# Casts of token weights handed out at other places, a second PSUM bank for outputs, and four tiles given over to float32 values

## The chip, the cores and the metric

The program runs on one core of one Trainium2 chip. The metric is the device time of one execution in microseconds (us). An execution is summed up below by its median over several runs; a profiled execution has a span (first to last instruction) and, a little longer, a time of its own.

A core has a matmul engine (PE) with its weight loads (PEld), the vector engine (DVE), the scalar engine (ACT), GpSimd (POOL) and a queue that issues most of the transfers (SP). Each engine works off its own list of instructions in order, so an instruction that waits holds back all that stand behind it in that list.

## The reference

Two stages are computed: a linear attention with a decay of its own for each head, and a mixer of two small networks, one over the tokens and one over the channels.

```python
# q, k, v: (4, 8, 768, 64), lam: (8,)
Dmask = np.where(rel >= 0, lam[:, None, None] ** rel[None, :, :], 0.0)
for b in range(nb):                       # blocks of 64 tokens
    intra = np.einsum('bhic,bhjc->bhij', qb, kb) * Dmask[None]
    intra = np.einsum('bhij,bhjd->bhid', intra, vb)
    inter = np.einsum('bhid,bhde->bhie', qb * lam_pow[None], kv_state)
    out[:, :, sl] = intra + inter
    kv_state = lam_block[None, :, None, None] * kv_state + np.einsum('bhsd,bhse->bhde', kb * rev_pow[None], vb)
...
x = out.transpose(0, 2, 1, 3).reshape(4, 768, 512)
h = np.maximum(x.transpose(0, 2, 1) @ w_tok1, 0.0) @ w_tok2      # w_tok1 768x256, w_tok2 256x768
u = x + h.transpose(0, 2, 1)
h2 = np.maximum(u @ w_ch1, 0.0) @ w_ch2                          # w_ch1 512x1536, w_ch2 1536x512
return (u + h2).astype(np.float32)
```

## The kernel before

**The order is written out by hand.** No scheduler moves anything: the order in which the Python code calls the engines is the order of their instructions. All waits between engines follow from the tiles that are written and read.

**First stage, attention with the token mixer (0 to about 206 us).** A loop runs over passes i = -2 ... 15 (L618); pass i works on pair i, two heads of one batch, and prepares the pairs behind it. A pass issues in this order:

- `scores(i+1)` on PE (L287, into `sc`), `weigh(i+1, 0)` on DVE (L300, `a` = scores times mask), `scale_q` on POOL (L241, `qs`);
- `outputs(i, 0)`: the first half of the pair's output on PE (L314 and L324, into the bank `xT`), copied by ACT into `uT` (L331);
- `state(i+1)`: `kv` on PE (L254), and DVE scans it into `sv` (L262); POOL later lays `sv` out as `stb` (L275), and ACT and POOL make `kd` for a later pair (L236);
- `weigh(i+1, 1)`, then `outputs(i, 1)`, the second half of the output, again into `xT` and copied by ACT;
- `turn_k(i+2)`: six transposes on PE in two groups (L211, banks `kt0` and `kt1`), each copied by ACT (L216); for early pairs the same for q (L228, L229), for later ones DVE turns q (L221);
- `work`, the token mixer's matmuls (`ph` L446, `pu` L467, with `hh`, `hl` and sums on ACT and DVE), and between its parts `turn_back(i, 0)` and `turn_back(i, 1)`: transposes `xp` on PE (L346), split by ACT into `xhi` (L354) and by DVE into `xlo` (L355).

**Banks.** PSUM has 8 banks here: `sc` has four, `xT` one, `sh` three. All that is called kv, kt, qt, xp, ph and pu takes the `sh` banks in turn, so each waits until the readers of the third one before it are done.

**Conversion steps.** The weights come as float64 words. Each piece is turned into float32 by a list of steps (`narrow`): two on ACT (L377, L378), three on DVE (L379, L380, L383), each on the result of the one ahead where they share a tile; then a split into a high and a low part: a cast on ACT, and a subtraction on POOL (`halves` L390 and L391 for token weights, `combine` L522 and `split_c2` L550 for channel weights). The steps stand in the queue `waiting`. `later(n)` takes up to n of them, one more where over seven wait, and stops ahead of the second ACT step (the third where n > 2; the first in the call after the second `turn_back`, if fewer than eight wait). It is called at set places of a pass: after `place()`, after each piece of work, and after each `turn_back`.

**Second stage (206 to 334 us) and third stage (334 us to the end)** are the channel mixer in a form with seven products in place of eight. In the third stage sums and products take their float32 values from a deque `temps` (nine tiles `t`, `snap`), and their split high and low parts from a deque `tiles` (eight halves of `tt`, and 12 of `hh0`, `hl0`, `hh1`, `hl1`). Both are used in rotation: the tile freed first is taken first. The steps there are `whole` (L837), `ramp` (L808), `hi_of` (L812), `low_sum` (L818), and the products L797 and L1052 on PE.

Of the kernel before, what the change touches and what calls it, by code (L numbers as in the profile page):

```python
# [25 lines left out]
def kernel(  # L26
# [41 lines left out]

    waiting = deque()

    def later(n, at_end=False):
        left = 0 if at_end and len(waiting) < 8 else 1 + (n > 2)
        n += len(waiting) > 7
        for _ in range(min(n, len(waiting))):
            left -= waiting[0] in acts
            if left < 0 and n < 99:
                break
            waiting.popleft()()

    acts = set()  # L80

    def act(f):
        acts.add(f)
        return f

# [220 lines left out]
    def outputs(i, g):  # L306
        b, p = pairs[i]
        st = stb[i % 2]
        xT = bank("xT", f"xT{i}{g}", 3 * P)
        for cg in range(3):  # L310
# [51 lines left out]

    def narrow(raw, a, sg, t=None):

        low, high = raw[:, :, 0], raw[:, :, 1]  # L370
        t = low if t is None else t
        af = a.bitcast(F32)
        top = sg.bitcast(F16).rearrange("p (n two) -> p n two", two=2)[:, :, 1]
        STT = nc.vector.scalar_tensor_tensor
        shr, shl, either = ALU.logical_shift_right, ALU.logical_shift_left, ALU.bitwise_or
        return [
            act(lambda: nc.scalar.activation(af, high.bitcast(F32), AF.Abs, scale=REBIAS)),  # L377
            act(lambda: nc.scalar.activation(top, high.bitcast(I32), AF.Copy, scale=VANISH)),  # L378
            lambda: STT(out=t, in0=low, scalar=29, in1=sg, op0=shr, op1=either),  # L379
            lambda: nc.vector.tensor_scalar(  # L380
                out=af, in0=af, scalar1=HIGH_MIN, scalar2=HIGH_MAX, op0=ALU.max, op1=ALU.min
            ),
            lambda: STT(out=a, in0=a, scalar=3, in1=t, op0=shl, op1=either),  # L383
        ]

    def halves(a, hi, lo, view):
        af = a.bitcast(F32)

        def split():
            nc.scalar.copy(out=hi, in_=view(af))  # L390
            nc.gpsimd.tensor_sub(out=lo, in0=view(af), in1=hi.bitcast(F32))  # L391

        return [act(split)]

# [24 lines left out]
    def convert_w2(i):  # L419
# [5 lines left out]
        lo = w2l.rearrange("p k s -> p (k s)")[:, ns]  # L425
        waiting.extend(narrow(raw[:, ns], tmp[:, :n], scr[:, 3072 : 3072 + n]))
        waiting.extend(halves(tmp[:, :n], hi, lo, lambda x: x))
# [82 lines left out]
    def combine(n, pool, a, pads=5):  # L510
# [13 lines left out]
        def low(w0, w1, src):  # L524
            nc.gpsimd.tensor_sub(out=of(1, w0, w1), in0=src, in1=of(0, w0, w1).bitcast(F32))  # L525

        return [
            act(lambda: high(0, 1, raw0)),
            act(lambda: high(1, 3, u1)),
            lambda: low(0, 1, raw0),  # L530
# [5 lines left out]
            *[lambda: None] * pads,  # L536
            act(lambda: high(3, 5, u0)),
            act(lambda: high(5, 7, u1)),
            lambda: low(3, 5, u0),
# [3 lines left out]
    def split_c2(n, pool, a):  # L543
# [10 lines left out]

        return [act(lambda: high(0)), act(lambda: high(1)), lambda: low(0), lambda: low(1)]

# [28 lines left out]
    def raw_operand(r, o, pool, eng, other):  # L585
# [5 lines left out]

        return [act(first), act(lambda: halve(r, o, 1, block(k, t + 1), other))]

# [24 lines left out]
    for i in range(-2, NI):  # L618
        if i == 0:
            nc.vector.memset(scr[:, 3072:], 0)  # L620
        if i == NP:
            all_of("w1", 3)
        if 0 <= i + 1 < NI:
            scores(i + 1)
# [25 lines left out]
        if place:  # L650
            place()
        later(1 if i >= 4 else 3)
        n = early.get(i, len(work) // 4)
        cuts = [0, n, max(n, (3 * len(work) + 1) // 4 if len(work) > 2 else len(work) // 2), len(work)]
        for n in range(3):
# [7 lines left out]
            if n < 2 and i >= 0:  # L663
                later(1 if i >= 4 else 3, n == 1)
        if 0 <= i + 3 < NI and i >= -1:
# [590 lines left out]
    for n in range(NQD):  # L1256
        r, g = divmod(n, NG)
        for s in range(7):
# [71 lines left out]
            else:  # L1330
# [6 lines left out]
                if n == NG + 1 and s == 1:  # L1337
                    for i in range(3):
                        for t in ("hh0", "hl0", "hh1", "hl1"):
                            tiles.append(hp.tile([P, CB], F32R, tag=t, name=f"{t}x{i}"))  # L1340
                    for t in ("c2h", "c2l"):
# [85 lines left out]
```

## Time and profile before

| what | us |
|---|---|
| median of 3 runs | 569.63 (568.62 to 572.48) |
| profiled execution, its own time | 567.56 |
| profiled execution, span | 565.8 |
| PE busy in the span | 541.0 |
| DVE, POOL, ACT busy | 387.8, 285.4, 247.3 |

A row of the timeline reads: start in us, duration, engine, line, operation, output from input, shape, count, and in brackets how long the engine was idle before it and what ended that. A row of the waits reads: who waited, for whom, in total, how often, and the longest. A row of windows gives the stretch, the busy time (and count) of each engine, the TensorE clock that was granted as a share of full speed, and the share and rate of the DMA engines. Names of tiles stand without their numbers.

The first stage is a mixture of short matmuls and of steps on four engines; in the second, PE has no idle time that the profile shows, and in the third nearly none.

### The profile page before, as it was taken

The page shows a single profiled execution, that of the slowest core. Times are in us where ns is not written, and L with a number is a line of the kernel's source. Part 1 is how long each engine was busy: PE and PEld are TensorE (multiplying, and loading weights), DVE is VectorE, ACT ScalarE, POOL GpSimd, SP SyncE. Part 2 cuts the span into 40 slices and gives each one's busy share as a digit, 9 for nine tenths or more (in the row PEclk, how much of TensorE's full clock was granted, in tenths as well). Part 3 has the DMA queues.
Part 4 walks back from the last instruction along what each step waited for, and adds up shares of the span by engine and source line. Part 5 has one row for each costly group of instructions (what it writes and reads, how often), then busy time and mean ns, then how long its engine had stood idle before and what let it go on. Part 6 is the DMA issues. An engine that isn't in the chain of part 4 may idle for free.

```text
span 565.8 us, 9630 instructions
## 1 busy us (share of the span) xinstructions
PE 541.0 (96%) x3686; PEld 459.9 (81%) x3686; DVE 387.8 (69%) x590; ACT 247.3 (44%) x449; POOL 285.4 (50%) x240
## 2 busy tenths in 40 slices
PE   5987989999999999999999999999998999999996
PEld 4877879988998988888888878888876888888884
DVE  4747776676684787888896667389479765575463
ACT  3456543453524546456445344343465334332111
POOL 6746548345324287667639753385788223131000
PEclk9989999999999999999999999999999999999999
DMA  9999887199630158687587999868536797653007
GB/s 183 248 228 209 189 192 170 30 228 216 133 71 2 74 205 311 221 286 279 189 294 238 259 213 252 308 218 311 181 104 223 156 234 280 240 182 137 0 3 146
DMA packets 163726, 108.12 MB, mean 191 GB/s; under 512 B 136800, under 2 KB 147552, under 8 KB 163680
## 3 DMA queue, kind: packets, MB, share of 16 engines
q1 hardware_dynamic: 153648, 87.31, 58.6%
q10 hardware_dynamic: 10032, 20.19, 9.7%
q8 instruction: 29, 0.48, 0.3%
q14 instruction: 17, 0.14, 0.1%
HBM read 75.50 MB, written 31.98 MB: 190 GB/s over the span
## 4 chain that ended last, share of the span: by engine, by line
PE 81%; DVE 6%; ACT 4%; issue 2%; DMA 2%; SPq 1%; POOL 1%; ACTq 1%; DVEq 0%; POOLq 0%
PE b L797 16%; PE po L998 11%; PE gb L1052 9%; PE d L797 8%; PE gc L1052 6%; PE ph L446 6%; PE pu L467 5%; PE a L797 4%; PE xT L314 4%; PE sc L287 3%; PE xT L324 2%; PE gb L998 2%; PE gc L998 2%; DMA qn<-in_q_dram 1%; PE xp L346 1%
## 5 line engine op out<-in xcount | busy, mean ns | idle before, releaser
L275 POOL COPY stb<-sv 64x320 f32<-64x320 f32 x32 | 25.4, 793 | 50.7 <-DVE sv L262 49.7
L314 PE MATMUL xT<-a,vn 128*64 128x128 f32 x384 | 37.1, 285 | 5.2 <-ACT uT L331 5.2
L331 ACT COPY uT<-xT 128x384 f32<-128x384 f32 x32 | 15.4, 480 | 55.5 <-PE xT L324 55.5
L1011 DVE TENSOR_TENSOR uT<-po,uT 128x512 f32<-128x512 f32 x48 | 32.6, 683 | 10.2 <-PE po L998 10.0
L998 PE MATMUL po<-hh,c2l 128*128 128x512 f32 x96 | 37.7, 393 | 0.0
L998 PE MATMUL po<-hl,c2h 128*128 128x512 f32 x96 | 37.6, 392 | 0.0
L998 PE MATMUL po<-hh,c2h 128*128 128x512 f32 x96 | 37.6, 391 | 0.0
L300 DVE TENSOR_TENSOR a<-sc,mask 128x384 f32<-128x384 f32 x64 | 32.1, 543 | 4.9 <-PE sc L287 4.9
L324 PE MATMUL xT<-qs,stb 128*64 128x128 f32 x320 | 32.0, 278 | 0.0
L818 POOL TENSOR_TENSOR tt<-t,tt 128x512 fp32r<-128x512 f32 x13 | 16.8, 1296 | 29.1 <-ACT tt L812 27.2
L314 PEld LDWEIGHTS xT<-a,vn 128*64 128x64 f32 x384 | 22.7, 139 | 9.3 <-ACT uT L331 6.0
L1067 DVE TENSOR_TENSOR uT<-gb,uT 128x512 f32<-128x512 f32 x40 | 26.1, 683 | 3.8 <-PE gb L1052 3.8
L446 PE MATMUL ph<-xhi,w1h 128*128 128x256 f32 x96 | 28.2, 294 | 0.3 <-DVE hl L451 0.3
L355 DVE TENSOR_TENSOR xlo<-xp,xhi 128x384 fp32r<-128x384 f32 x32 | 17.7, 554 | 14.7 <-ACT xhi L354 14.6
L287 PE MATMUL sc<-qT,kT 64*128 64x128 f32 x384 | 26.5, 286 | 0.8 <-DVE qT L221 0.5
L446 PE MATMUL ph<-xlo,w1h 128*128 128x256 f32 x96 | 27.1, 283 | 0.0
L446 PE MATMUL ph<-xhi,w1l 128*128 128x256 f32 x96 | 27.1, 283 | 0.0
L287 PEld LDWEIGHTS sc<-qT,kT 64*128 64x128 f32 x384 | 23.4, 193 | 3.9 <-issue 1.7
L525 POOL TENSOR_TENSOR c1l<-wa,c1h 128x512 fp32r<-128x512 f32 (+1 forms) x12 | 18.7, 1569 | 15.6 <-ACT c1h L522 15.6
L818 POOL TENSOR_TENSOR hl1x<-t,hh1x 128x512 fp32r<-128x512 f32 x12 | 16.8, 1404 | 18.9 <-ACT hh1x L812 18.3
L241 POOL TENSOR_TENSOR qs<-qT,lamp 128x640 f32<-128x640 f32 x16 | 25.4, 1589 | 0.0
L797 PE MATMUL b<-o,c1h 128*128 128x512 f32 x72 | 25.2, 391 | 0.0
(359 smaller groups left out, 1724.8 us busy)
## 6 DMA issues: line engine op xcount, KB each, us to landing
c1h<-k SPq DMA_DIRECT2D x12, 896.0 KB, 5.6
c1l<-k SPq DMA_DIRECT2D x12, 896.0 KB, 8.1
raw<-in_moe_w_ch_dram SPq DMA_DIRECT2D x7, 1024.0 KB, 6.0
kn<-in_k_dram SPq DMA_DIRECT2D x32, 192.0 KB, 4.5
vn<-in_v_dram SPq DMA_DIRECT2D x16, 384.0 KB, 5.8
k<-c1h ACTq DMA_DIRECT2D x6, 896.0 KB, 3.6
k<-c1l ACTq DMA_DIRECT2D x6, 896.0 KB, 4.2
out_dram<-y SPq DMA_DIRECT2D x80, 64.0 KB, 2.4
```

Of the source, the lines that this page charges most:

```text
L287: nc.tensor.matmul(out=sc[h][:, c * P : (c + 1) * P], lhsT=kTs[i][r, cs], rhs=qTs[i][r, cs], start=True, stop=True,)
L300: nc.vector.tensor_mul(out=a, in0=scored[i, g][h].rearrange("p (c i) -> p c i", i=P), in1=mask[:, 2 * p + h, None, :].broadcast_to([P, 3, P]),
L314: nc.tensor.matmul(out=xT[h * D : (h + 1) * D, cs], lhsT=vns[i][:, h, c, :], rhs=weights_of[i, g, h][:, cg, :], start=(cg == 0), stop=False,)
L324: nc.tensor.matmul(out=xT[h * D : (h + 1) * D, cs], lhsT=st[:, c - 1, h, :], rhs=qss[i][:, c - 1, :], start=False, stop=(cg == 2),)
L446: nc.tensor.matmul(out=ph, lhsT=w[:, c, fs], rhs=x[:, c], start=(i == 0), stop=(i == 3 * NC - 1))
L467: nc.tensor.matmul(out=pu, lhsT=h[:, kk, cs], rhs=w[:, kk, ss], start=(i == 0), stop=(i == 3 * NK - 1))
L797: nc.tensor.matmul(out=c[into], lhsT=w[:, WI[o], ct], rhs=x[:, ct], start=(first and i == 0), stop=(i == 5), skip_group_check=True,)
L818: nc.gpsimd.tensor_sub(out=B_[key][1], in0=src, in1=B_[key][0].bitcast(F32))
L998: nc.tensor.matmul(out=po, lhsT=w[:, jj, cs], rhs=h, start=(i == 0), stop=(i == 3 * JG - 1), skip_group_check=n >= NG)
L1011: nc.vector.tensor_add(out=ub, in0=two(po), in1=ub)
L1052: nc.tensor.matmul(out=G[into, t], lhsT=w2[:, v, j, t * P : (t + 1) * P], rhs=x, start=(o in (5, 1, 2) and not second and i == 0), stop=(i ...
L1067: nc.vector.tensor_add(out=ub, in0=two(G[into, t]), in1=ub)
```

## The change

Five things are edited:

1. `later` is rewritten. One more step is taken where more than 4 wait (more than 7, and in pass 6 more than 30, once all six token pieces are done). The number of ACT steps allowed is now given by the caller: three after `place()` in passes below 4. `hold` is set in the calls after the two `turn_back`s in passes below 4 (except the second of pass 3) and after the second one in later passes. With it a step that is marked as a cast is not taken while fewer than eight wait; once all six token pieces are done, that holds for every ACT step.
2. The casts of token and channel weights are marked (`act(..., True)`).
3. `outputs(i, 1)` takes an `sh` bank in place of the `xT` bank.
4. The second and third piece of `w_tok2` get an empty step behind their two ACT steps.
5. In the third stage the last set of `hh0`, `hl0`, `hh1`, `hl1` goes to `temps` as float32 and not to `tiles`: 13 and 16 in place of 9 and 20.

```diff
-    waiting = deque()
-
-    def later(n, at_end=False):
-        left = 0 if at_end and len(waiting) < 8 else 1 + (n > 2)
-        n += len(waiting) > 7
+    waiting, spare = deque(), 7
+
+    def later(n, on_act=1, hold=False):
+        n += len(waiting) > (spare if len(ready) == 6 else 4)
         for _ in range(min(n, len(waiting))):
-            left -= waiting[0] in acts
-            if left < 0 and n < 99:
+            f = waiting[0]
+            on_act -= f in acts
+            if n < 99 and (on_act < 0 or hold and f in (casts if len(ready) < 6 else acts) and len(waiting) < 8):
                 break
             waiting.popleft()()
...
     def outputs(i, g):
         b, p = pairs[i]
         st = stb[i % 2]
-        xT = bank("xT", f"xT{i}{g}", 3 * P)
+        xT = bank("sh" if g else "xT", f"xT{i}{g}", 3 * P)
...
             act(lambda: nc.scalar.activation(top, high.bitcast(I32), AF.Copy, scale=VANISH)),
+            *pads,
             lambda: STT(out=t, in0=low, scalar=29, in1=sg, op0=shr, op1=either),
...
-        return [act(split)]
+        return [act(split, True)]
...
-        waiting.extend(narrow(raw[:, ns], tmp[:, :n], scr[:, 3072 : 3072 + n]))
+        waiting.extend(narrow(raw[:, ns], tmp[:, :n], scr[:, 3072 : 3072 + n], None, [lambda: None] * (i > 0)))
...
+        spare = 30 if i == 6 else 7
...
-        later(1 if i >= 4 else 3)
+        later(*((1,) if i >= 4 else (4, 3)))
...
             if n < 2 and i >= 0:
-                later(1 if i >= 4 else 3, n == 1)
+                later(*((1, 1, n == 1) if i >= 4 else (3, 2) if (i, n) == (3, 1) else (2, 1, True)))
...
                         for t in ("hh0", "hl0", "hh1", "hl1"):
-                            tiles.append(hp.tile([P, CB], F32R, tag=t, name=f"{t}x{i}"))
+                            at = dict(tag=t, name=f"{t}x{i}")
+                            if i < 2:
+                                tiles.append(hp.tile([P, CB], F32R, **at))
+                            else:
+                                temps.append(hp.tile([P, CB], F32, **at))
```

PE's own list keeps its order; only the bank of `outputs(i, 1)` and the names of tiles in the third stage differ. ACT, DVE and POOL have the same instructions in another order in passes 1 to 10, and after that the same order with other tiles. Three places matter below. Lines above some 70 are four to ten higher in the changed file.

**ACT, from the turn-back of pass 1 to that of pass 2.** Before (L377 and L378 are conversion steps, L354 `xhi`, L236 `kd`, L390 the cast of a token weight, L331 the copies of the output, L216 and L229 those of k and q):

```order
L377 ACTIVATE uT<-uT 128x512
L378 ACTIVATE scr<-uT 128x512
L354 CAST xhi_334<-xp_453 128x3x128
L236 ACTIVATE kd_459<-kn_235,mask 128x320
L390 CAST w1h<-uT 128x512
L354 CAST xhi_334<-xp_466 128x3x128
L331 COPY uT<-xT_505 128x384
L331 COPY uT<-xT_534 128x384
L216 COPY kT_549<-kt_550 128x384
```

The same place in the changed kernel:

```order
L381 ACTIVATE uT<-uT 128x512
L382 ACTIVATE scr<-uT 128x512
L358 CAST xhi_334<-xp_455 128x3x128
L240 ACTIVATE kd_461<-kn_235,mask 128x320
L358 CAST xhi_334<-xp_464 128x3x128
L335 COPY uT<-xT_503 128x384
L335 COPY uT<-xT_532 128x384
L220 COPY kT_547<-kt_548 128x384
L220 COPY kT_547<-kt_553 128x384
L233 COPY qT_546<-qt_558 128x384
L233 COPY qT_546<-qt_563 128x384
L395 CAST w1h<-uT 128x512
```

The cast moved from between the two `xhi` of pass 1 to behind the copies of pass 2.

**ACT, from the first turn-back of pass 3 to the outputs of pass 4.** Before:

```order
L354 CAST xhi_575<-xp_690 128x3x128
L236 ACTIVATE kd_696<-kn_474,mask 128x320
L390 CAST w1h<-uT 128x512
L377 ACTIVATE uT<-uT 128x512
L354 CAST xhi_575<-xp_703 128x3x128
L331 COPY uT<-xT_741 128x384
```

In the changed kernel:

```order
L395 CAST w1h<-uT 128x512
L381 ACTIVATE uT<-uT 128x512
L382 ACTIVATE scr<-uT 128x512
L358 CAST xhi_575<-xp_689 128x3x128
L240 ACTIVATE kd_695<-kn_472,mask 128x320
L395 CAST w1h<-uT 128x512
L358 CAST xhi_575<-xp_702 128x3x128
L381 ACTIVATE uT<-uT 128x512
L382 ACTIVATE scr<-uT 128x512
L335 COPY uT<-xT_743 128x384
```

Two casts of this piece of the list now stand here, the first of them behind the copies of pass 3, and both ACT steps of the next weight stand ahead of the copies of pass 4.

**DVE at the same place.** Before (L379, L380 and L383 are conversion steps, L355 `xlo`, L300 `a`, L262 `sv`):

```order
L379 SCALAR_TENSOR_TENSOR uT<-uT,scr 128x512
L380 TENSOR_SCALAR uT<-uT 128x512
L355 TENSOR_TENSOR xlo_576<-xp_690,xhi_575 128x3x128
L383 SCALAR_TENSOR_TENSOR uT<-uT 128x512
L355 TENSOR_TENSOR xlo_576<-xp_703,xhi_575 128x3x128
L300 TENSOR_TENSOR a_737<-sc_719,mask 128x384
L300 TENSOR_TENSOR a_739<-sc_720,mask 128x384
L262 SCALAR_TENSOR_TENSOR sv_764<-keep,kv_753 128x320
```

In the changed kernel:

```order
L384 SCALAR_TENSOR_TENSOR uT<-uT,scr 128x512
L359 TENSOR_TENSOR xlo_576<-xp_689,xhi_575 128x3x128
L385 TENSOR_SCALAR uT<-uT 128x512
L388 SCALAR_TENSOR_TENSOR uT<-uT 128x512
L359 TENSOR_TENSOR xlo_576<-xp_702,xhi_575 128x3x128
L384 SCALAR_TENSOR_TENSOR uT<-uT,scr 128x512
L304 TENSOR_TENSOR a_739<-sc_721,mask 128x384
L304 TENSOR_TENSOR a_741<-sc_722,mask 128x384
L266 SCALAR_TENSOR_TENSOR sv_766<-keep,kv_755 128x320
```

The first DVE step of the next weight (L384) came ahead of the weighing and of `sv`.

**DVE in the third stage**, at the place that stands at 419 to 425 us of the trace, where the operands of the last token blocks are made. Before (L837 adds into a `temps` tile, L808 is `ramp`, L583 makes low parts of operands):

```order
L583 TENSOR_TENSOR o7l_4527<-uT,o7h_4526 128x512
L837 TENSOR_TENSOR snap_3667<-d_4498,t_3661 128x512
L808 SCALAR_TENSOR_TENSOR t_3660<-snap_3667,t_3660 128x512
L583 TENSOR_TENSOR o5l_4552<-uT,o5h_4551 128x512
L808 SCALAR_TENSOR_TENSOR hl0x_3904<-snap_3667,hh0x_3903 128x512
```

In the changed kernel:

```order
L588 TENSOR_TENSOR o7l_4527<-uT,o7h_4526 128x512
L843 TENSOR_TENSOR t_3660<-d_4498,snap_3666 128x512
L814 SCALAR_TENSOR_TENSOR hl0x_3904<-t_3660,hl0x_3904 128x512
L588 TENSOR_TENSOR o5l_4552<-uT,o5h_4551 128x512
L814 SCALAR_TENSOR_TENSOR tt_3707<-t_3660,tt_3707 128x512
```

The order is the same; the addition writes another tile.

More of the change, by code (lines that the diff above doesn't have):

```diff
@@ L80, with act @@
     acts = set()
-    def act(f):
+    casts = set()
+    def act(f, cast=False):
         acts.add(f)
+        if cast:
+            casts.add(f)
         return f
@@ L361, with narrow @@
     w2l = tokw.tile([P, NK, S], F32R, name="w2l")
-    def narrow(raw, a, sg, t=None):
+    def narrow(raw, a, sg, t=None, pads=()):
         low, high = raw[:, :, 0], raw[:, :, 1]
@@ L527, in combine @@
         return [
-            act(lambda: high(0, 1, raw0)),
-            act(lambda: high(1, 3, u1)),
+            act(lambda: high(0, 1, raw0), True),
+            act(lambda: high(1, 3, u1), True),
             lambda: low(0, 1, raw0),
@@ L536, in combine @@
             *[lambda: None] * pads,
-            act(lambda: high(3, 5, u0)),
-            act(lambda: high(5, 7, u1)),
+            act(lambda: high(3, 5, u0), True),
+            act(lambda: high(5, 7, u1), True),
             lambda: low(3, 5, u0),
@@ L553, in low @@
             nc.gpsimd.tensor_sub(out=c2s[n][1][:, j], in0=a[:, j], in1=c2s[n][0][:, j].bitcast(F32))
-        return [act(lambda: high(0)), act(lambda: high(1)), lambda: low(0), lambda: low(1)]
+        return [act(lambda: high(0), True), act(lambda: high(1), True), lambda: low(0), lambda: low(1)]
     def block(k, t):
@@ L590, in first @@
             halve(r, o, 0, block(k, t), eng)
-        return [act(first), act(lambda: halve(r, o, 1, block(k, t + 1), other))]
+        return [act(first, True), act(lambda: halve(r, o, 1, block(k, t + 1), other), True)]
     groups = deque()
```

## The prediction

> **What bounds the kernel now.** I read the page's engines first, then PE's waits, then the timelines of ACT, DVE and PE around each wait, and the windows for the granted clock.
>
> ```profile
> PE 541.0 (96%) x3686; PEld 459.9 (81%) x3686; DVE 387.8 (69%) x590; ACT 247.3 (44%) x449; POOL 285.4 (50%) x240
> ...
> PE kt L211 <- DMA kn<-in_k_dram: 5.7, 1, 5.7
> PE xT L314 <- ACT uT L331: 5.2, 4, 2.1
> PE xp L346 <- DVE sv L262: 1.3, 1, 1.3
> PE pu L467 <- DVE xlo L355: 1.2, 1, 1.2
> PE gc L1052 <- DVE hl0x L808: 1.0, 1, 1.0
> PE xp L346 <- DVE uT L472: 1.0, 1, 1.0
> PE pu L467 <- DVE sv L262: 0.9, 1, 0.9
> ```
>
> PE is busy for 96% of the span, and the change gives it the same matmuls in the same order. What can be won is PE's idle time (565.8 - 541.0 = 24.8 us) and time at a lower clock. The 5.7 us at the start are the first load and stay. The change is aimed at the rest, above all at 5.2 us in which `outputs(i, 1)` waits for ACT's copy out of the only `xT` bank. The question is what is late next at each of these places.
>
> **The change part by part: the bank and the casts, pass 2.**
>
> ```profile
> 30.92:34.34 3.42, 1.43 (x34) 1.29 (x30) 2.32 (x5) 1.91 (x5) 0.63 (x1) 1.00 1.14 229
> 34.34:37.76 3.42, 3.32 (x27) 2.99 (x28) 2.82 (x6) 0.49 (x2) 3.36 (x4) 0.50 0.98 182
> 44.00:48.00 4.00, 3.12 (x36) 2.56 (x36) 3.81 (x7) 2.37 (x7) 3.94 (x4) 1.00 1.34 232
> ...
> 33.01 0.62 ACT L390 CAST w1h<-uT 128x512 fp32r<-128x512 f32 x1 [1.51 <-DVE uT L383]
> 33.90 0.48 ACT L331 COPY uT<-xT 128x384 f32<-128x384 f32 x1
> ...
> 32.28 0.69 DVE L383 SCALAR_TENSOR_TENSOR uT<-uT 128x512 uint32<-128x512 uint32 x1
> 34.04 0.56 DVE L355 TENSOR_TENSOR xlo<-xp,xhi 128x384 fp32r<-128x384 f32 x1 [1.06 <-ACT xhi L354]
> 34.51 1.01 DVE L300 TENSOR_TENSOR a<-sc,mask 128x384 f32<-128x384 f32 x2
> 35.44 0.81 DVE L262 TENSOR_TENSOR_SCAN sv<-keep,kv 128x320 f32<-128x320 f32 x1
> ...
> 34.44 0.69 PE L314 MATMUL xT<-a,vn 128*64 128x128 f32 x4 [2.09 <-ACT uT L331]
> 37.20 1.13 PE L211 MATMUL kt<-ident,kn 128*128 128x128 f32 x6
> 39.81 1.61 PE L287 MATMUL sc<-qT,kT 64*128 64x128 f32 x24
> 44.59 0.44 PE L314 MATMUL xT<-a,vn 128*64 128x128 f32 x4 [1.35 <-ACT uT L331]
> ...
> 112.99 0.44 PE L314 MATMUL xT<-a,vn 128*64 128x128 f32 x4
> ...
> 114.45 0.88 PE L211 MATMUL kt<-ident,kn 128*128 128x128 f32 x6
> ```
>
> The first window is the stretch with the longest wait, the second what follows (the clock is the third number from the end): 0.50 for 3.42 us, so this wait costs 2.1 us and then half of 3.4, 1.7 us. The wait of 1.35 us in pass 3 left it at 1.00 (third window). Its cause: the cast waits 1.51 us for L383, and `xhi`, the copy of `xT` and, through `xlo`, the weighing and `sv` stand behind it. Without the cast there, L383 is one `xlo` earlier (start to start 0.47) and ends at 32.5; two `xlo` take 0.94, the two `a` 0.93, `sv` 0.81: it ends at 35.2 in place of 36.25. That is the next thing late. With `outputs(i, 1)` in the `sh` banks, `kt1` gets the bank of `kv` and must wait for `sv`; before, only the third user after `kv` did. `kt0` is a group of three of the six transposes, some 0.4 us. `outputs(2, 1)` itself takes the bank of an `xp` and waits for the first `xlo`, to 33.0; such a half output takes 1.46 us (112.99 to 114.45 in a later pass), so `kt0` stands at 34.5 and `kt1` at 35.2, where it was 37.2 + 0.4 = 37.6 or a little more. Gain 2.5 us, clock included.
>
> **Pass 3** has the same shape (the wait of 1.35): `kt1` will again wait for `sv`, which is earlier by less, since the cast held back now stands ahead of L377 there. Between 0 and -1.35; I take -0.6, nearer to 0, since DVE's chain stays whole.
>
> **Pass 4** is where I expect a new wait.
>
> ```profile
> 47.96 0.78 ACT L378 ACTIVATE scr<-uT 128x512 f16<-128x512 int32 x1
> 50.90 0.62 ACT L390 CAST w1h<-uT 128x512 fp32r<-128x512 f32 x1 [1.38 <-DVE uT L383]
> 51.42 0.65 ACT L377 ACTIVATE uT<-uT 128x512 f32<-128x512 f32 x1
> 51.98 0.46 ACT L354 CAST xhi<-xp 128x384 fp32r<-128x384 f32 x1
> ...
> 52.95 1.01 DVE L300 TENSOR_TENSOR a<-sc,mask 128x384 f32<-128x384 f32 x2
> 53.87 0.81 DVE L262 TENSOR_TENSOR_SCAN sv<-keep,kv 128x320 f32<-128x320 f32 x1
> ...
> 48.26 1.61 PE L287 MATMUL sc<-qT,kT 64*128 64x128 f32 x24 [0.54 <-DVE qT L221]
> 50.94 0.75 PE L254 MATMUL kv<-vn,kd 128*64 128x64 f32 x20
> 54.33 0.87 PE L211 MATMUL kt<-ident,kn 128*128 128x128 f32 x6
> ```
>
> The second `xhi` ended 4.2 us after the scores began (52.44 - 48.26) and will again: one cast more (0.62) is ahead of it, one L377 less (0.65). But behind it ACT now does L377 and L378 of the next weight, and DVE does its L379 (0.69, as L383 above) ahead of `a`. So `a` begins 0.65 + 0.78 + 0.69 less some 0.2 of overlap, 1.9 us, after `xhi`, where it was 52.95 - 52.44 = 0.5. `sv` ends 1.4 us later against the scores: 6.4 + 1.4 = 7.8. PE, which no longer waits for ACT there, would be ready for `kt1` 5.2 us after the scores (kv's end, 51.69 - 48.26 = 3.4, plus 1.46 and 0.4). It stands idle 2.6 us, and `kt1` comes at 7.8 where it came at 6.5: +1.4. The idle stretch is longer than the 2.1 that brought the half clock, so I add the same 1.7. Bounds: from 0 (ACT runs ahead) to +3.1; I take +3.1.
>
> [...]
>
> **Passes 5, 6, 9, 10.**
>
> ```profile
> 63.41 1.30 DVE L380 TENSOR_SCALAR uT<-uT 128x512 f32<-128x512 f32 x1
> 80.95 1.23 DVE L379 SCALAR_TENSOR_TENSOR scr<-scr 128x1024 uint32<-128x1024 uint32 x1 [1.28 <-ACT scr L378]
> 106.61 1.37 ACT L378 ACTIVATE scr<-uT 128x1024 f16<-128x1024 int32 x1
> 113.33 0.80 DVE L262 TENSOR_TENSOR_SCAN sv<-keep,kv 128x320 f32<-128x320 f32 x1
> ```
>
> Pass 5: one L383 goes behind `sv` (-0.6), and L380 may lose its stretch (1.30 here); `kt1` takes over the wait of `xp` (1.3), with 0.4 less work ahead of it. Between -1.3 and +0.4; taken -0.7. Pass 6: `xlo` comes ahead of the 1.23 us L379 rather than behind it and the sums between the steps, which shortens the waits of 1.2 and 1.0; DVE stays full there, so -0.9 of 2.2. Pass 9: ahead of the L378 at 106.6 now come a cast (0.6), two `xhi` (0.4 each), `kd` (0.4) and a double-width L377 (1.0): it starts at 109.4 and ends at 110.8. L379 (1.2), `hl` and L380 (taken as 0.9; the nearest row, L383's, has 0.69 for one step) and L383 (1.2) follow ahead of `a` (0.9) and `sv` (0.8), which ends at 115.8, not at 114.1; `kt1`, due at 114.45 + 0.4, waits: +1.0, between 0 and +1.6. Pass 10: L383 goes behind `sv`, which takes the wait of 0.9, less what a sum behind it holds up: -0.6.
>
> **Where the bank is free of all this.** In pass 15 nothing lies between the two outputs, so 0.6 us go; in eleven other passes PE starts within 0.05 us of the copy's end:
>
> ```profile
> 112.46 0.48 ACT L331 COPY uT<-xT 128x384 f32<-128x384 f32 x1 [2.41 <-PE xT L324]
> ...
> 180.16 0.44 PE L314 MATMUL xT<-a,vn 128*64 128x128 f32 x4 [0.58 <-ACT uT L331]
> ```
>
> The copy ends at 112.94, the `xT` of pass 9 starts at 112.99. What this costs a pass lies between 0 and some 0.15; I take 0.1, so -1.1. In these passes `sv` ends about 0.7 us ahead of `kt1` (114.13 against 114.85 here), so the bank costs nothing; that cover goes where DVE is late, as in passes 4 and 9.
>
> **The third stage.**
>
> ```profile
> 419.08 1.84 POOL L1127 TENSOR_TENSOR c2lx<-snap,c2lx 128x512 fp32r<-128x512 f32 x1
> 420.95 0.69 DVE L837 TENSOR_TENSOR snap<-d,t 128x512 f32<-128x512 f32 x1 [1.19 <-POOL c2lx L1127]
> ```
>
> DVE waits 1.19 us to overwrite a `temps` tile that POOL still reads; PE's waits for `hl0x` (1.0) and two smaller ones follow. With 13 tiles in rotation the addition takes one that was freed earlier. DVE is full from there on, so all that follows comes 1.2 us earlier and no more: -1.2, between 0 and -2.2. With four fewer `tiles`, writers could wait for PE; the halves freed last are several matmul groups old, so 0, at worst +1.
>
> **What else moves.** With the casts go POOL's subtractions (L391, L525, L553), now behind `stb`. POOL is busy for half the span and their first readers are matmuls of pass 4 and of the second stage: 0; if that cover goes, at most one such step, 1.84 by the row above. On SP one store of a converted piece (L506), which waits for DVE, now stands behind the loads of two pairs' k, q and v and of a weight piece, so these start earlier; the only load in the list of PE's waits above is the first one, at the start: 0 either way. The empty steps cost nothing by themselves.
>
> **The sum.** -2.5 - 0.6 + 3.1 - 0.7 - 0.9 + 1.0 - 0.6 - 0.6 - 1.1 - 1.2 = -4.1 us on the profiled execution: span 561.7, its own time 567.56 - 4.1 = 563.5. That execution was 2.1 us under the median of the runs shown; from the median, 569.63 - 4.1 = 565.5.
>
> **The rivals.**
> - *The clock stays full in pass 4*: -4.1 - 1.7 = -5.8, 563.7. [...] Against it: 2.1 us brought 0.50. Its chance is 0.20. [...]
> - *DVE and ACT run clear of each other*: no new wait in passes 4 and 9 (their +4.1 gone): -8.2, 561.4. For it: ACT is busy 44%; against: L377 to L379 stand ahead of `a` in the list. 0.14.
> - *The waits only change their names*: `kt1` waits for `sv` wherever `xT` waited for the copy, and passes 5, 6 and 10 win nothing: of the sum stay pass 2 (-2.5), +3.1, +1.0, the -0.6 of pass 15 and -1.2: -0.2, 569.4. For it: in pass 2 `sv` (36.25) ended 1.9 us after the copy (34.38). 0.18.
> - *Slower*: `kt1` waits for `sv` in every pass. It takes `sv` 0.7 us later than now before it costs anything; were it 1.2 us late in each of 13 passes, that is 13 x 0.5 = +6.5 on top of -4.1, 572.0, and it decides against the change from 0.7 + 4.1/13 = 1.0 us on. Against it: after pass 10 the order of DVE does not change. 0.08.
>
> My forecast has the remaining 0.40.
>
> **How the numbers follow.** 1% is 5.7 us, about what a measurement of this kernel can tell from no change: faster means under 563.9, slower over 575.3. The forecast is 565.5; its own range 563 to 567.5. Faster: all of the second rival (0.14), half of the first (0.11), a fifth of the forecast (0.08): 0.33. Slower: part of the last, 0.05. Within 1%: 0.62. The range of 560.5 to 570.0 leaves out the last rival and the outer ends of the second and third, about 0.18.
>
> **What would show it.** Right: no wait of `xT` for `uT` in PE's waits; a `kt` wait for `sv` of about 2.6 us in pass 4 (near 50 to 53 us), with a window at clock 0.50 behind it; the scores of pass 4 about 3 us earlier than 48.26, those of pass 5 at 58 to 60; no wait of DVE for `c2lx`. Wrong: the scores of pass 3 not 2 us earlier than 39.81; `kt` waiting for `sv` in passes 12 to 14; ACT or DVE waiting for PE's reads of `tiles` in the third stage.

## The result and the profile after

| | before | after |
|---|---|---|
| median, 22 runs each | 569.76 us | 567.0 us |
| lowest and highest | 565.91 to 574.35 | 563.68 to 575.35 |
| ratio after / before | | 0.995, 95% interval 0.9927 to 0.9973 |
| profiled execution, its own time | 567.56 | 569.58 |

The changed kernel is faster by half a per cent, -2.8 us between the medians, and the interval leaves out 1. Its profiled execution is one of its longer ones: of the 22 times ten lie from 563.7 to 565.4, none between 565.4 and 566.9, and the others above. That of the kernel before, 567.56, is one of its shorter (four of its 22 runs lie below it). So the page below says two things at once, what the change does and what makes a run long, and the experiments have to part them. Against the profile before, this one is 1.2 us shorter up to the first `b` of the second stage (200.69 in place of 201.93), 3.4 us longer from there to DVE's step `o` at 415.37 before and 417.50 here (216.8 against 213.4), and 0.1 us shorter behind that.

The page's engines and the waits of PE in the changed kernel (lines are four to six higher than before: `sv` is L266, `uT`'s copy L335, `kt` L215):

```profile
PE 540.6 (95%) x3686; PEld 458.0 (81%) x3686; DVE 387.8 (68%) x590; ACT 246.1 (43%) x449; POOL 288.0 (51%) x240
...
PE kt L215 <- DMA kn<-in_k_dram: 5.5, 1, 5.5
PE kt L215 <- DVE sv L266: 3.0, 3, 1.4
PE b L803 <- ACT p L836: 2.2, 1, 2.2
PE kv L258 <- DMA vn<-in_v_dram: 1.3, 1, 1.3
PE pu L472 <- DVE uT L477: 0.9, 2, 0.5
PE gc L1058 <- DVE tt L814: 0.9, 1, 0.9
PE kt L215 <- ACT uT L335: 0.8, 1, 0.8
```

The 5.2 us in which `xT` waited for `uT` are gone. New are 3.0 us of `kt` behind `sv`, a wait for a transfer of v, and one of 2.2 us in the second stage.

**Pass 2** in the timelines of ACT and PE and in the windows (the clock is third from the end):

```profile
30.87 0.66 ACT L381 ACTIVATE uT<-uT 128x512 f32<-128x512 f32 x1 [2.91 <-DMA uT<-in_moe_w_tok_dram]
31.43 0.76 ACT L382 ACTIVATE scr<-uT 128x512 f16<-128x512 int32 x1
32.06 0.45 ACT L358 CAST xhi<-xp 128x384 fp32r<-128x384 f32 x1
32.42 0.56 ACT L240 ACTIVATE kd<-kn,mask 128x320 f32<-128x320 f32 x1
...
32.26 0.30 PE L258 MATMUL kv<-vn,kd 128*64 128x64 f32 x2 [1.30 <-DMA vn<-in_v_dram]
33.03 0.90 PE L258 MATMUL kv<-vn,kd 128*64 128x64 f32 x18 [0.47 <-ACT kd L240]
34.50 0.69 PE L318 MATMUL xT<-a,vn 128*64 128x128 f32 x4 [0.57 <-DVE xlo L359]
...
30.15:33.57 3.42, 1.65 (x35) 1.30 (x32) 1.31 (x3) 2.70 (x6) 0.00 (x0) 1.00 0.71 160
33.57:36.98 3.41, 2.83 (x32) 2.59 (x27) 3.41 (x8) 0.16 (x1) 0.35 (x1) 0.50 1.22 230
```

ACT sat 2.91 us in front of the first token weight, whose load landed at 30.85 us (29.35 in the profile of before; from issue to landing it took 10.0 us here and 8.6 there), and `xhi` and `kd` stood behind it. PE lost 2.3 us in three short waits and then ran 3.4 us at half clock. The wait of `xT` is gone, and the pass is no shorter.

**The second stage.** One row of ACT before, one after:

```profile
291.10 1.14 ACT L550 CAST c2h<-wa 128x512 fp32r<-128x512 f32 x2 [0.72 <-DMA k<-c2h]
```

```profile
295.98 1.14 ACT L555 CAST c2h<-wa 128x512 fp32r<-128x512 f32 x2 [4.89 <-DMA k<-c2h]
297.02 0.58 ACT L836 COPY p<-b 128x512 f32<-128x512 f32 x1
```

The cast overwrites a tile that is still being written to DRAM. That write took 5.0 us to land before and 9.1 us here; PE's `b` waited 2.2 us for the copy behind the cast. In the profiles below it took from 3.1 to 9.1 us: 9.1 also with only the `temps` edit (e3_temps), where nothing ahead of it is changed, and not over 5.3 in e5_late_w1, e6_both, e7_early_kd, e9_thirds and e10_sv_first, which hold the whole change. So the change is neither needed for a late write nor enough for one.

**By passes.** The distance from the first matmul of one pass's scores (`sc` in PE's timeline) to the next pass's. The column e4 is the experiment e4_no_temps, bank and casts without the `temps`, in whose profile the weights landed at 29.77 us.

| pass | before | after | e4 | e4 less before | forecast |
|---|---|---|---|---|---|
| 2 | 11.03 | 11.40 | 8.33 | -2.70 | -2.5 |
| 3 | 8.45 | 7.84 | 7.84 | -0.61 | -0.6 |
| 4 | 11.85 | 12.70 | 12.73 | +0.88 | +3.1 |
| 5 | 12.16 | 12.71 | 12.71 | +0.55 | -0.7 |
| 6 | 14.47 | 13.33 | 13.33 | -1.14 | -0.9 |
| 9 | 11.64 | 13.02 | 13.02 | +1.38 | +1.0 |
| 10 | 12.71 | 12.77 | 12.72 | 0.0 | -0.6 |
| 0, 1, 7, 8, 11 to 15 (up to the first `b` of the second stage) | 105.54 | 103.09 | 103.29 | -2.25 | -1.7 |
| sum | 187.86 | 186.87 | 183.98 | -3.88 | -2.9 |

Outside pass 2 the two profiles agree within 0.2 us in a row: that is the change. In pass 2 they differ by 3.1 us; that this is the landing, e9_thirds below shows. The table begins with pass 0. Ahead of it e4's profile lost 0.7 us (the scores of pass 0 began at 14.75, before at 14.07, in the changed kernel at 13.82), since the first 24 score matmuls of the program took 2.93 us in it, 2.33 before and 2.02 in the changed kernel. So its first `b` came 3.2 us earlier than before, and not 3.9.

### The profile page after: what moved, and what is told of

Read it like the earlier page. It is cut to its first block, busy times and chain, and to the rows that moved or that the text cites. A ratio compares the mean times of both kernels' runs of the same rounds, so it can differ in the third digit from the quotient of the medians.

```text
span 567.8 us, 9622 instructions
## 1 busy us (share of the span) xinstructions
PE 540.6 (95%) x3686; PEld 458.0 (81%) x3686; DVE 387.8 (68%) x590; ACT 246.1 (43%) x449; POOL 288.0 (51%) x240
## 4 chain that ended last, share of the span: by engine, by line
PE 65%; DVE 11%; DMA 10%; ACT 6%; issue 2%; POOL 2%; SPq 2%; ACTq 0%; DVEq 0%
PE b L803 13%; PE gb L1058 9%; PE gc L1058 7%; PE d L803 6%; PE ph L451 5%; DMA raw<-in_moe_w_ch_dram 5%; PE pu L472 4%; PE po L1004 3%; PE xT L318 3%; PE a L803 3%; PE sc L291 2%; PE xT L328 2%; PE gb L1004 2%; PE gc L1004 2%; DMA qn<-in_q_dram 2%
## 5 line engine op out<-in xcount | busy, mean ns | idle before, releaser
L335 ACT COPY uT<-xT 128x384 f32<-128x384 f32 x32 | 15.2, 480 | 51.5 <-PE xT L328 51.4
L824 POOL TENSOR_TENSOR hl1x<-t,hh1x 128x512 fp32r<-128x512 f32 x7 | 9.3, 1333 | 39.8 <-ACT hh1x L818 39.8
L803 PE MATMUL a<-o,c1h 128*128 128x512 f32 x72 | 25.2, 391 | 0.0
```

Of the source, the lines that this page charges most:

```text
L803: nc.tensor.matmul(out=c[into], lhsT=w[:, WI[o], ct], rhs=x[:, ct], start=(first and i == 0), stop=(i == 5), skip_group_check=True,)
```

## The experiments

The first four take the change apart.

**e1_bank**: the kernel before with

```diff
-        xT = bank("xT", f"xT{i}{g}", 3 * P)
+        xT = bank("sh" if g else "xT", f"xT{i}{g}", 3 * P)
```

> The kernel before with the second PSUM bank for outputs alone. Theory (the gain of the change needs bank and casts together): xT never waits for uT, but the casts still stand ahead of the second xhi, so in pass 2 the third transpose group kt1 waits for sv, which ends near 36.25 us as before; the scores of pass 3 come about 1 us earlier than 39.81, the half clock stays, passes 3 and 4 win half of their 1.35 and 1.2 us: about -2 us, 0.996. Rival (the bank alone is the change): all of the measured 0.995 or better, scores of pass 3 at 37 to 38. Second rival (waits only change names): 1.000, every lost wait found again as kt1 behind sv.

Measured 0.998 (0.9949 to 1.0011). The first row of PE's waits that isn't the start:

```profile
PE kt L211 <- DVE sv L262: 6.6, 5, 1.9
```

The bank alone changes 5.2 us behind ACT into 6.6 us behind `sv`. The scores of pass 3 came at 39.52, 0.3 us earlier; the half clock left pass 2 and came in pass 5 instead, behind the wait of 1.9 us (that pass took 14.01 us, 12.16 before). By its waits this is the rival in which waits only change their names, with 0.2 us won in each pass that has no conversions; the interval holds the theory's 0.996 as well. The weights landed late in this profile too (ACT waited 2.68 us for them), so its pass 2, 11.44 us, does not show what the bank alone does there.

**e2_casts**: the changed kernel with these parts undone:

```diff
-        xT = bank("sh" if g else "xT", f"xT{i}{g}", 3 * P)
+        xT = bank("xT", f"xT{i}{g}", 3 * P)
...
-                            if i < 2:
-                                tiles.append(hp.tile([P, CB], F32R, **at))
-                            else:
-                                temps.append(hp.tile([P, CB], F32, **at))
+                            tiles.append(hp.tile([P, CB], F32R, **at))
```

> The kernel before with the new hand-out of conversion steps alone (casts not at a pair's end, the one step per place in pair seven, the empty steps), one xT bank and the old tiles. Theory: xT goes on waiting for ACT's copy; in pass 2 the copy comes one cast (0.6 us) earlier, passes 5 and 6 win about 1 us together, pass 9 loses up to 1: between -1.5 and +0.5, 0.999. Rival (the casts carry the gain): 0.995 and no wait of xT for uT over 0.5 us. Second rival (more conversion work collides later): slower than before by 1 to 3 us, 1.002 to 1.005.

Measured 0.999 (0.9962 to 1.0019), as the theory had it. Pass 2 took 8.63 us without a half clock, so the gain there belongs to the casts. Pass 4 took 14.16 (+2.3): `xT` still waits 1.5 us for ACT there, and `ph` 0.8 us for `sv`. With the bank (e4) that pass costs 0.9. The casts need the bank in pass 4, the bank needs the casts in pass 5 (14.01 us in e1_bank, 12.71 in e4); for pass 2 no profile has the bank without the casts and with the weights on time.

**e3_temps**: the kernel before with the last hunk of the change alone (four tiles to `temps`).

> The kernel before with the four tiles given to float32 temps alone. By the forecast's term: DVE's wait of 1.19 us for c2lx near 421 us goes and the third stage ends 1.2 us earlier: 0.998. Theory after the first look at the changed kernel: the wait goes, but DVE then runs beside POOL and one of its scalar_tensor_tensor steps takes 1.7 to 1.8 us in place of 0.68, so the distance from the first o (L583) at 415 to the transposes near 438 shrinks by 0.2 us at most: 1.000 within 0.001.

Measured 1.0003 (0.9968 to 1.0037), an interval that holds 0.998 too; the trace decides. DVE's timeline in the third stage, then the last of these steps in the kernel before (`hl0x` there, `tt` here), and then POOL's and DVE's in the changed kernel:

```profile
423.53 0.68 DVE L837 TENSOR_TENSOR t<-d,snap 128x512 f32<-128x512 f32 x1
424.31 1.00 DVE L808 SCALAR_TENSOR_TENSOR hl0x<-t,hl0x 128x512 f32<-128x512 f32 x1
425.42 1.60 DVE L583 TENSOR_TENSOR o5l<-uT,o5h 128x512 fp32r<-128x512 f32 x1
426.95 1.77 DVE L808 SCALAR_TENSOR_TENSOR tt<-t,tt 128x512 fp32r<-128x512 f32 x1
```

```profile
424.35 0.68 DVE L808 SCALAR_TENSOR_TENSOR hl0x<-snap,hh0x 128x512 fp32r<-128x512 f32 x1
```

```profile
424.71 1.74 POOL L1133 TENSOR_TENSOR c2hx<-t,c2hx 128x512 fp32r<-128x512 f32 x1
...
425.22 1.78 DVE L814 SCALAR_TENSOR_TENSOR tt<-t,tt 128x512 fp32r<-128x512 f32 x1
```

The wait of 1.19 us for `c2lx` is gone, and the `tt` step, which took 0.68 us before, takes 1.77: 1.1 us are given back three steps behind the addition. The changed kernel shows why: POOL's addition runs to 426.45, DVE's step began inside it and ends at 427.00, 0.55 us behind it. From DVE's step `o` that waits 2.18 us for ACT (415.37 before, 417.50 after, 419.21 here) to the end of the span it is 150.4, 150.3 and 150.3 us. The term of -1.2 measured -0.1.

**e4_no_temps**: the changed kernel with that hunk undone.

> The changed kernel without its float32 temps (bank and casts together, the third stage as before). Theory: 0.995 to 0.996 of before, the same as the changed kernel within 0.001, since the temps alone measured 1.000; in the third stage DVE waits 1.2 us for c2lx again and PE's last three waits (some 2.5 us together) are of the same sum as with the temps. The forecast's term for the temps (-1.2 us) would make it 0.002 slower than the changed kernel: 0.997. On pass 2 this is a second look at bank and casts together: if the weights land near 30.8 us again, ACT waits for them 2 us or more, kv of pass 2 waits for vn, and pass 2 takes over 11 us; if they land near 29.4 us, pass 2 takes 8.6 us or less and the clock stays 1.00.

Measured 0.9941 (0.9909 to 0.9973), 564.74 us in the middle. The parts alone sum to 0.997, both together lie a little lower, within the intervals. Pass 2, in ACT's timeline and in the window of the whole pass:

```profile
29.79 0.68 ACT L381 ACTIVATE uT<-uT 128x512 f32<-128x512 f32 x1 [0.70 <-DMA uT<-in_moe_w_tok_dram]
...
29.24:37.57 8.33, 7.53 (x107) 6.47 (x107) 5.23 (x10) 5.22 (x12) 3.33 (x4) 1.00 0.94 190
```

The load landed 0.5 us behind the start of the scores (29.24), in the changed kernel's profile 2.7 us behind (28.11). Here the change does what the forecast said of pass 2.

Five more ask what holds pass 2.

**e8_fill**: the kernel before, PE kept busy where it waited, by transposes into unused columns of the bank of `kv` (`bk`).

```diff
+        if i == 3:
+            for _ in range(12):
+                nc.tensor.transpose(out=bk[:, 384:512], in_=ident, identity=ident)
```

> The kernel before with 12 transposes of the identity put behind kv of pass 2, into unused columns of the kv bank, where PE sat idle for 2.1 us; nothing else. Theory (the lower clock follows PE's idle share in the stretch before, and cost 1.7 us): PE's wait for the uT copy shrinks to 0.5 us or less, the clock stays 1.00 from 34 to 38 us, and the scores of pass 3 come 9.3 us after those of pass 2 (11.0 before): 1.7 us less, 0.997. Rival (the half rate comes from something else, such as the DMAs at that time): the clock is 0.50 for 3.4 us all the same, or comes at the next wait (1.35 us, pass 3), 1.000.

Measured 0.997 (0.9938 to 1.0002). PE's timeline and the windows:

```profile
33.01 1.53 PE L264 MATMUL kv<-ident 128*128 128x128 f32 x12
35.17 0.44 PE L318 MATMUL xT<-a,vn 128*64 128x128 f32 x4 [0.63 <-ACT uT L335]
...
34.00:38.00 4.00, 3.37 (x40) 2.81 (x39) 3.13 (x6) 2.37 (x7) 3.50 (x3) 1.00 0.96 186
38.00:42.00 4.00, 4.00 (x65) 3.56 (x65) 1.86 (x4) 2.86 (x7) 1.85 (x2) 1.00 1.02 194
```

The waited-for copy comes no earlier, and yet pass 2 takes 9.98 us in place of 11.03, at full clock; no other window of the first stage is at 0.50. With PE's idle time filled, the half clock did not come. This is one profile, and the interval of the runs reaches 1.0002. (Less than 1.7 us was won because the weights landed 1.1 us after the start of the scores, 30.09 against 29.01, where it was 0.6 before: the copy came 0.5 us later.)

**e5_late_w1**: the changed kernel, the first conversion steps a pass later.

```diff
     def later(n, on_act=1, hold=False):
+        if i == 1 and len(ready) < 3:
+            return
```

> The changed kernel, with no conversion step handed out in the second pair's turn, so the first steps on the token weights come one pass later. Theory (in the profiled run of the changed kernel ACT waited 2.9 us for the landing of the weights at 30.87 us, and xhi, kd and with them kv and xT of pass 2 stood behind it; that wait, not the bank, leaves the half clock there): ACT waits for no weights in pass 2, the clock is 1.00 from 28 to 40 us, the scores of pass 3 come 7.5 to 9 us after those of pass 2 (11.4 in the changed kernel), and the time is 2 to 4 us under the changed kernel: 0.989 to 0.992 of before. Rival (the same steps crowd passes 3 and 4): pass 2 is short, but passes 3 to 5 are longer by as much: 0.995. Second rival (vn lands late all the same): kv of pass 2 still waits 1.3 us for vn.

Measured 0.993 (0.9899 to 0.996), between theory and rival. Pass 2 took 7.98 us with no wait for the weights. But POOL's subtractions now stand ahead of `kd`, and pass 4 took 14.35 us, with a half clock behind the longer of these two waits:

```profile
PE kv L260 <- POOL kd L242: 3.3, 2, 2.1
...
46.83:50.24 3.41, 1.35 (x36) 1.31 (x36) 2.44 (x5) 2.00 (x4) 2.04 (x2) 1.00 0.82 149
50.24:53.65 3.41, 3.41 (x25) 2.86 (x22) 3.41 (x7) 2.33 (x5) 2.29 (x2) 0.50 1.05 206
```

**e6_both** and **e7_early_kd**: `kd` scaled ahead of `stb` and of the steps; e6 on top of e5_late_w1, e7 on the changed kernel.

```diff
+        if i + 2 < NI:
+            scale_k(i + 2)
         if place:
             place()
...
-            if n == 0 and i + 2 < NI:
-                scale_k(i + 2)
```

> The changed kernel with the conversion steps one pass later (as in e5_late_w1) and with kd of the next pair scaled ahead of the stb copies and of the steps handed out with them. Theory: in e5_late_w1 kd waited behind POOL's subtractions (kv waits 2.1 and 1.2 us in passes 4 and 5, and the first of them brought a half clock of 3.4 us); with kd first both waits go and no half clock comes before the end: 2.1 + 1.2 + 1.7 = 5.0 us under e5_late_w1, some 0.984 to 0.987 of before, scores of pair 15 at 160 to 161 us (165.47 in e5_late_w1). Rival (what stands behind kd is late next): stb, now a kd (1.1 us) later, makes xT wait for stb, or kt waits for sv 1 to 1.5 us in each of passes 4 to 6: then no more than 2 us under e5_late_w1, 0.990.

> The changed kernel with kd scaled ahead of the stb copies and steps, its conversion steps where they are. Theory (pass 2 hangs on the landing of the weights): the waits of kv for kd in passes 2 and 3 (0.5 and 0.6 us) go, ACT still waits for the weights in pass 2 and xhi and the uT copy behind it; pass 2 stays over 10.5 us when the weights land after 30 us, and the time is about 1 us under the changed kernel: 0.993. Rival (kd is what holds pass 2): pass 2 takes under 9 us with the weights late, 0.988 or less.

Both missed: 0.9951 (0.9921 to 0.9981), and 1.0014 (0.9979 to 1.005). In the first pairs POOL makes both halves of `kd`, and here it waited for a mask before it began them. `stb`, which in the changed kernel began at once behind `sv` (12.53), now stood behind `kd` and began 3.6 us after `sv`'s end. POOL, and PE in pass 0, in e7:

```profile
14.60 2.14 POOL L240 TENSOR_SCALAR kd<-kn,mask 128x320 f32<-128x320 f32 x2 [2.82 <-DVE mask L175]
16.68 1.54 POOL L279 COPY stb<-sv 64x320 f32<-64x320 f32 x2
...
17.47 0.43 PE L328 MATMUL xT<-qs,stb 128*64 128x128 f32 x2 [1.01 <-POOL stb L279]
18.28 0.32 PE L328 MATMUL xT<-qs,stb 128*64 128x128 f32 x1 [0.37 <-POOL stb L279]
```

Pass 0 took 9.12 us in both (7.20 in the changed kernel). In e6 the waits for `kd` went as expected, but `kt` waited 2.5 us for `sv` in pass 4 with a half clock behind it: 15.75 us.

**e9_thirds**: the changed kernel, the landing itself moved. The first weight is loaded in three pieces, the second and third behind `load_v(3)`.

```diff
-    def load_w1():
+    def load_w1(i):
+        cs = slice(2 * i, 2 * i + 2)
         nc.sync.dma_start(
-            out=words(3).rearrange("p (c f) -> p c f", c=NC),
-            in_=w_tok1.bitcast(U32).rearrange("(c s) f -> s c f", s=P),
+            out=words(3).rearrange("p (c f) -> p c f", c=NC)[:, cs],
+            in_=w_tok1.bitcast(U32).rearrange("(c s) f -> s c f", s=P)[:, cs],
         )
...
+        if i == 0:
+            load_w1(1)
+            load_w1(2)
...
         if i == -1:
-            load_w1()
+            load_w1(0)
```

> The changed kernel with the load of the first token weight in three pieces of 512 KB: the first where the whole was, the other two behind the load of v of the fourth pair. Theory (where the changed kernel is slow in pass 2, PE has run ahead to a landing that the bank cannot make earlier): the first piece lands before 27 us and v before 31 us, ACT and kv of pass 2 wait for no DMA, pass 2 takes 8.4 us or less in the profile with the clock at 1.00; against the changed kernel's profile 3 us less there, and against its runs about 1.5 us less in the middle: 0.992. Rival (the landing is not what splits the runs): pass 2 is long again or the same time is lost in passes 3 and 4 where the later pieces are read, 0.995.

Measured 0.9905 (0.9867 to 0.9943), as the theory had it. ACT in pass 2, and the window of the pass:

```profile
27.72 0.70 ACT L381 ACTIVATE uT<-uT 128x512 f32<-128x512 f32 x1
28.29 0.80 ACT L382 ACTIVATE scr<-uT 128x512 f16<-128x512 int32 x1
28.93 0.48 ACT L358 CAST xhi<-xp 128x384 fp32r<-128x384 f32 x1
...
28.00:36.45 8.45, 7.61 (x107) 6.36 (x107) 5.75 (x10) 5.16 (x12) 3.32 (x4) 1.00 1.05 243
```

The scores of pass 2 began at 28.00, as early as in the changed kernel's profile, and the pass took 8.45 us in place of 11.40, at full clock: ACT waits for no load there, and `kv` for no `vn` (that wait, 1.3 us, comes in pass 4, which takes 12.70 us all the same). The highest run was still 570.4, so the landing is not all that makes a run long.

The last three try what is left.

**e10_sv_first**: the changed kernel with `weigh(i + 1, 0)` moved behind `state(i + 1)`.

```diff
             scale_q(i + 1)
-            weigh(i + 1, 0)
...
         if 0 <= i + 1 < NI:
+            weigh(i + 1, 0)
             weigh(i + 1, 1)
```

> The changed kernel with sv ahead of the first two a on DVE in each pass (all four a behind it). Theory (the price of the second bank is kt1's wait for sv): sv ends up to 0.9 us earlier where DVE is late, so the waits of kt for sv in passes 5, 9 and 10 (1.15, 1.4, 0.5 us) shrink to 0.5, 0.5 and 0: some 2 us less than the changed kernel, 0.991 or 0.992. Rival (a becomes late): xT or the scores wait for a in every pass, by up to 0.5 us, or sv, now waiting for kv with nothing before it, idles DVE and xlo and hl come later: 0.995 to 1.000.

Measured 0.9914 (0.988 to 0.9947). Pass 5 went from 12.71 to 11.85 and pass 9 from 13.02 to 12.08, a step of 0.9 each; pass 4 went up by 0.6 (13.27), since `kt` waits 1.9 us for `sv` there, which it does not in the changed kernel. Pass 0 went up by 0.7 (7.92 against 7.20; 7.88 in e12_two). All passes but pass 2 sum to 0.4 us less than in the changed kernel's profile, not to the theory's 2, so they do not explain a ratio that came out where the theory had it.

**e11_keep**: the changed kernel with the writes of `c2h` and `c2l` two products earlier.

```diff
-            if 1 <= n <= NG and s == 6:
+            if 1 <= n <= NG and s == 4:
                 keep_c2(n - 1)
```

> The changed kernel with the write of c2h and c2l to DRAM in the second stage issued two products earlier. Theory (the waits of b for ACT at 238 and 298 us in the changed kernel's profile, 2.9 us together, come from a write that took 9.1 us to land in place of 4 to 5 and stood behind nothing of the change): no wait of PE for p or u over 0.5 us between 200 and 330 us; runs over 567 us become rarer; the middle of the runs 0.5 to 1 us lower than the changed kernel's, 0.993 to 0.994. Rival (the writes are as late two products earlier, or push the other writes of ACT's queue): the wait is found elsewhere in the second stage and the time is the same, 0.995.

A miss: 1.0021 (0.9992 to 1.005), slower than the changed kernel. From the first `b` to DVE's same step `o` (420.58) its profile took 222.2 us, the changed kernel's 216.8. The waits went elsewhere in the second stage:

```profile
PE po L1004 <- DVE uT L1017: 3.3, 3, 2.2
...
PE po L1004 <- POOL c2l L558: 1.1, 1, 1.1
```

Why the write takes 3 us in one execution and 9 in another stays open.

**e12_two**: e9_thirds and e10_sv_first together.

> The changed kernel with both edits that brought something: the first token weight loaded in three pieces, and sv ahead of all four a on DVE. Theory (the two are different terms: the landing in pass 2, and kt1's wait for sv in passes 5 and 9): they add, pass 2 at 8.4 us or less with the clock at 1.00, pass 5 at 11.9, pass 9 at 12.1, pass 4 at 13.3 (sv waits there all the same): 1.2 us under the pieces alone, 0.988 of before. Rival (both lower the same slack on DVE): no better than the better of the two, 0.990 to 0.991.

Measured 0.9915 (0.9877 to 0.9953), 564.33 us in the middle: the rival's number, for another reason (the interval still holds the theory's 0.988). Pass 9 kept its gain (12.08), and in pass 4 this happened, in PE's timeline and the windows:

```profile
52.95 0.55 PE L215 MATMUL kt<-ident,kn 128*128 128x128 f32 x3 [2.60 <-DVE sv L266]
...
50.98:54.39 3.41, 1.44 (x12) 1.44 (x13) 3.41 (x6) 0.97 (x3) 2.01 (x3) 1.00 1.24 237
54.39:57.80 3.41, 3.41 (x18) 3.41 (x17) 2.66 (x5) 0.89 (x2) 0.40 (x2) 0.50 1.03 103
```

Pass 4 took 14.77 us. With e10_sv_first alone the same wait was 1.94 us and the clock stayed full. The three lowest ratios, 0.9905 to 0.9915, are those of e9_thirds, e10_sv_first and e12_two: all below the changed kernel's 0.995, though the intervals still overlap with its own and do not part the three. Nor are the three shown to be ahead of e4_no_temps and e5_late_w1: the medians of all five lie between 564.3 and 564.8 us, and their ratios differ mainly because the kernel before had medians of 567.7 and 568.2 beside those two and of 569.9 to 570.2 beside these three.

## Why the prediction was right, and where it was not

The forecast of 565.5 us met the median of 567.0 within its own range, and "within 1%" was the likeliest case. It was right in sum by errors of both signs.

- **Passes 2, 3, 6 and 9** held: -2.5, -0.6, -0.9, +1.0 against -2.70, -0.61, -1.14, +1.38. For pass 2 this is true only where the weights land on time. The forecast read the wait of `xT` back to ACT and ACT's back to the cast, but not this row of ACT, in the kernel before:

```profile
29.37 0.68 ACT L377 ACTIVATE uT<-uT 128x512 f32<-128x512 f32 x1 [0.75 <-DMA uT<-in_moe_w_tok_dram]
```

  ACT waited for the load even then. The forecast put the loads at 0 since PE's list of waits names only the first one; it did not ask for which loads ACT waits. In the changed kernel's profile the scores of pass 2 began 0.7 us earlier (28.11 against 28.78) and the load landed 1.5 us later, and the wait for it took the gain of the pass. e9_thirds, whose scores begin as early and whose ACT waits for no load, has the gain. Why the load takes 8.6 us in one execution and 10.0 in another stays open. By the forecast's own marks the profiled execution reads as a miss (scores of pass 3 at 39.51, and not 2 us ahead of 39.81) and e4 as a hit (37.57). What this adds to the median cannot be read from single profiles; it points the right way for a median 1.5 us above the forecast.
- **Pass 4** is the term that failed: +3.1 forecast, +0.88 measured. The chain ahead of it was right, and even too short: `sv` ended 9.0 us after the scores, against 7.8 in the forecast. But `kt1` did not get the bank of `kv` there. PE, DVE and POOL in pass 4 of the changed kernel:

```profile
53.68 0.55 PE L215 MATMUL kt<-ident,kn 128*128 128x128 f32 x3 [0.83 <-ACT uT L335]
...
52.96 1.74 DVE L384 SCALAR_TENSOR_TENSOR uT<-uT,scr 128x512 uint32<-128x512 uint32 x1 [0.71 <-ACT scr L382]
54.62 1.01 DVE L304 TENSOR_TENSOR a<-sc,mask 128x384 f32<-128x384 f32 x2
55.55 0.81 DVE L266 TENSOR_TENSOR_SCAN sv<-keep,kv 128x320 f32<-128x320 f32 x1
...
52.61 1.53 POOL L245 TENSOR_TENSOR qs<-qT,lamp 128x640 f32<-128x640 f32 x1
```

  It waited for the copy of the second output, at 53.68, and ran 2.7 us ahead of `sv`'s end (56.36). The forecast counted the `sh` banks as strictly every third, as the description of the kernel has it. In this pass the program gives `kt1` the bank of the second output: `kt1` was written 1.9 us before `sv` began to read `kv`. What the pass lost are shorter waits, `kt1`'s of 0.8 us (0.4 in e4) and one of 0.4 us of the transposes `xp` for `hl`. The event itself is real: it came in e12_two, where `kt1` does wait for `sv`, with 2.60 us and the half clock, as priced (pass 4 there is 2.9 us longer than before).
- **Passes 5 and 10** were to win 1.3 and won nothing (+0.55, 0.0). `kt1` took over the wait (1.15 and 0.5 us), as said, but DVE was as late as before, and what comes behind (`xlo` for `ph` 0.6 us, the sum for `pu` 0.4 us) waits again. Here the rival of waits that change names was right.
- **The bank where nothing else is late** brought 0.2 us a pass, not 0.1: -2.25 in place of -1.7.
- **The third stage** was to win 1.2 and won 0.1. DVE's wait went, and a step that then ran beside POOL (1.77 us in e3_temps and 1.78 in the changed kernel, 0.68 before) took the time back.
- **Slower by waits for `sv` in every pass** did not come: three such waits, 3.0 us in all.

With the weights on time the terms ahead of the second stage sum to -3.9, where the forecast had -2.9, and the third stage adds -0.1, where it had -1.2: -4.0 against -4.1. That these sums agree is luck: pass 4 and the bank came out 2.8 us better than forecast, passes 5 and 10 and the third stage 3.0 us worse.

## What to carry to other kernels

When a wait is taken away, ask of each engine behind it what it waited for already: the transfer or the step with the smallest slack is the next floor, whatever PE does. A bank or a tile added to a rotation renames waits as long as the reader is the late one; move the reader (here `sv`: 0.9 us won in each of two passes, 0.6 and 0.7 lost in two others) or the landing. And two or three microseconds of idle PE can cost more than themselves (here 3.4 us at half clock behind some of them), so price a wait with the clock behind it.

## What the runs showed of the hardware

- **DVE beside POOL.** Between 417 and 446 us, in three profiles (before, after, e3_temps), each of the 24 DVE steps over 0.8 us with both operands in SBUF ended 0.55 us behind the POOL operation that ran when it began; alone such a step takes 0.68 (`hl0x` at 424.35 in the profile before). In pass 4 it is the same: `qs` runs from 52.61 to 54.14, and L384, which began inside it, ends at 54.70. What holds the step until then, no trace here shows.
- **The clock.** In the eight profiles with a half clock in the first stage it lasted 3.4 us, and PE was busy for 28 to 48% of the 3.4 us ahead of it (0.94 of 3.41 in e6_both, 1.65 of 3.42 in the changed kernel). The length of the wait does not decide: 1.85 us (e1_bank) brought it, 1.94 (e10_sv_first) and 1.97 (e7_early_kd, pass 2) did not. Nor does the busy share of such a stretch alone: behind 1.43 us busy of 3.42 (30.92 to 34.34 before) the half clock came, behind 1.43 of 3.40 (33.00 to 36.40 in e7_early_kd) it did not. Why nearly equal waits differ, no run here shows.
